# Talking-heads attention with an expert layer: stores of converted weights three slots later, two maxima taken a step later

## The chip, the cores and the metric

The kernel runs on one core of a Trainium2 chip. A core has five engines that run their own instruction queues in order: TensorE (PE, matmuls; PEld its weight loads), VectorE (DVE), ScalarE (ACT), GpSimd (POOL) and SyncE (SP). SP computes nothing here: it issues nearly all DMAs, one after the other, and where one of them has to wait for its data or for room, everything behind it in SP's queue waits too. The metric is the device time of one execution in microseconds (us).

## The reference

Inputs are q, k, v of shape (4 batches, 12 heads, 448 rows, 64), two 12 x 12 matrices that mix heads, and the two weights of the second layer, which arrive as 64-bit floats.

```python
scores = scale * np.matmul(q, k.transpose(0, 1, 3, 2))
scores = np.einsum('bhij,hg->bgij', scores, w_pre)     # mix the heads
scores = scores - np.max(scores, axis=-1, keepdims=True)
attn = np.exp(scores)
attn = attn / (np.sum(attn, axis=-1, keepdims=True) + 1e-09)
attn = np.einsum('bhij,hg->bgij', attn, w_post)        # and again
x = np.matmul(attn, v)                                 # -> (1792, 768)
h = x @ w_in                                           # 768 x 2048
g = np.where(h >= 1, h, np.where(h <= -1, 0.0, (h + 1) ** 2 / 4))
out = g @ w_out                                        # 2048 x 768
```

## The kernel before

**Three stages.** First attention (to about 495 us), then the product with `w_in` and the gate g (to 710.6), then the product with `w_out`. The instructions are issued in an order that the program writes out by hand (`tc.manual_schedule()`): each engine runs its instructions in the order in which the Python code emits them, and a framework adds the waits for data and for free buffers.

**Attention.** A batch's 448 rows are cut into row tiles of 120, 120, 120 and 88 rows. `scores` (L157) multiplies q by k for all heads, ScalarE and VectorE copy the result to `ssb` (L162, L166), and a DMA regroups it (`load_s`, L181, SBUF to SBUF) into blocks of 10 rows x 12 heads, so that mixing heads becomes one 120 x 120 matmul (`pre`, L200 and L202). Every second block is split into a high and a low part by VectorE first (`split`, L189). Then come the row maximum (VectorE, L205), the exponential (ScalarE, L211), the norm (L217, L218 on VectorE, L222 on POOL), the second mixing (`post`, L232, evicted by ScalarE at L234) and the product with v (`pv`, L249). The loop at the end of the attention stage goes over 48 groups, three to a row tile, mostly of four blocks. In each iteration n it emits, in this order: the score loads of group n+1; `pre`, maxima, exponentials and norm of group n; a burst of conversion slots; `post` of group n-1; a row tile's transposes, `pv` and `scores`; loads of k, q and v for later; a second burst of conversion slots. Twelve groups make a batch: v of the next batch is loaded during some of them, k during others.

**The conversion of the weights** runs in these bursts, in groups 2 to 42. The weights are cut into 64 chunks of 128 x 384. For each, `load` (L327) brings the 64-bit floats (384 KB) into `wraw`, of which there are three buffers. Five steps make 32-bit floats in a tile `wt`: step 0 and step 1 on ScalarE (L288 into `wt`, L294 into `wk`), step 2 and 3 on VectorE (L297, L303), step 4 on POOL, an add (L307). `store` (L334) writes the 192 KB back to HBM. A slot is one entry of a list of closures; chunk n begins in slot 3n, and the table `lags` says how many slots later each step comes:

```python
lags = ((store, 8), (4, 6), (2, 4), (3, 4), (1, 3), (0, 2), (load, 0))
```

So the add of chunk n is emitted in slot 3n+6 and its store in 3n+8. Within a slot the order is that of the table. All DMAs named so far are SP's.

**The second stage** is 56 steps j = 7q + k: eight groups q of seven products k = 0 to 6, the first four groups with 512 columns, the others with 384. A step is 18 matmuls (`product`, L509) into one of the accumulators in PSUM named X, Y and Z. Per step the loop emits: the matmuls; `split_w(j + 2)`, which splits the weights of two steps later into a high part (ScalarE, L399) and a low one (VectorE, L402); a gate, in four of the seven steps; sums of weights and x (L435, L464), splits of x (L456, L457); and at the end `evict_f(j)`, which takes the accumulator to SBUF: a copy on ScalarE for k = 0, 2, 3 (L562), an add on VectorE for k = 1, 4, 5 (L564). The matmuls of step k = 6 add to the accumulator that was evicted at k = 4, and therefore wait for that add.

**The gate** g is computed as max(h, f(h)). With `act=True` (k = 3 and k = 4, from the second group on) ScalarE does three operations into a temporary (L536, L543, L544), two temporaries taking turns, and VectorE takes the maximum (L547). VectorE's queue holds the maximum right there, ahead of the sums, splits and evictions of the same step.

Of the kernel before, what the change touches and what calls it, by code (L numbers as in the profile page):

```python
# [9 lines left out]
F32 = mybir.dt.float32  # L10
F32R = mybir.dt.float32r
I32 = mybir.dt.int32
# [3 lines left out]
ALU = mybir.AluOpType  # L16
# [6 lines left out]
def tile_talking_heads_moe(  # L23
# [11 lines left out]
    nc = tc.nc  # L35
# [13 lines left out]
    CW = 384  # L49
# [25 lines left out]
    for b in range(B):  # L75
        for i0 in range(0, S, QT):
            n = min(QT, S - i0)
# [194 lines left out]
    def convert(st, p):  # L272

        def halves():  # L280
            w = st["raw"].bitcast(I32).rearrange("p (n t) -> p n t", t=2)
            return w[:, :, 0], w[:, :, 1]

        def scaled():
            lo, hi = halves()
            if "t" not in st:
                st["t"] = p.tile([128, CW], I32, tag="wt", name="wt", bufs=3)
            nc.scalar.activation(out=st["t"].bitcast(F32), in_=hi.bitcast(F32), func=AF.Copy,  # L288
                                 scale=2.0 ** -111)

        def lowest():
            lo, hi = halves()
            st["k"] = p.tile([128, CW], I32, tag="wk", name="wk", bufs=2)
            nc.scalar.activation(out=st["k"], in_=lo.bitcast(U32), func=AF.Copy, scale=2.0 ** -29)  # L294

        def shifted():
            nc.vector.tensor_single_scalar(out=st["t"], in_=st["t"], scalar=3,  # L297
                                           op=ALU.logical_shift_left)

        def sign():  # L300
            lo, hi = halves()
            t = st["t"]
            nc.vector.scalar_tensor_tensor(out=t, in0=hi, scalar=-0x80000000, in1=t,  # L303
                                           op0=ALU.bitwise_and, op1=ALU.bitwise_or)

        def add():
            nc.gpsimd.tensor_tensor(out=st["t"], in0=st["t"], in1=st.pop("k"), op=ALU.add)  # L307

        return [scaled, lowest, shifted, sign, add]

    def conv_units():
        chunks = []
        for f in range(NF):
            for c in range(2):
                chunks.append((w_in[c * CW:(c + 1) * CW, f * 128:(f + 1) * 128]
                               .rearrange("(k p) f -> p k f", p=128), wsd[f, c]))
            for c in range(2):
                chunks.append((w_out[f * 128:(f + 1) * 128, c * CW:(c + 1) * CW],
                               wod[f, :, c * CW:(c + 1) * CW]))
        st = {}  # L320
        us = []

        def load(n):
            raw = qp.tile([128, CW], I64, tag="wraw", name="wraw", bufs=3)
            src = chunks[n][0]
            dst = raw if len(src.shape) == 2 else raw.rearrange("p (k f) -> p k f", f=128)
            nc.sync.dma_start(out=dst, in_=src)  # L327
            st[n] = {"raw": raw}
            st[n]["steps"] = convert(st[n], qp)

        def store(n):
            dst = chunks[n][1]
            src = st.pop(n)["t"].bitcast(F32)
            nc.sync.dma_start(out=dst, in_=src)  # L334


        lags = ((store, 8), (4, 6), (2, 4), (3, 4), (1, 3), (0, 2), (load, 0))
        for slot in range(3 * len(chunks) + 8):
            def unit(slot=slot):
                for f, lag in lags:  # L340
                    n, rest = divmod(slot - lag, 3)
                    if rest == 0 and 0 <= n < len(chunks):
                        if callable(f):
                            f(n)
                        else:
                            st[n]["steps"][f]()
            us.append(unit)
        return us


    NA = 1024
    NH = (512, 384)
# [6 lines left out]
    raw = {}  # L359
    wts = {}  # L360
    xraw = {}
    xop = {}
    gq = {}
    named = {}
    area = {"gg": 16544, "xd": 82080, "xc": 122848, "xa": 147424}

    def view(p, off, *dims, dt=F32):
        n = 1
        for d in dims:
            n *= d  # L370
        named[p] = named.get(p, -1) + 1
        x = nc.alloc_sbuf_tensor_at(f"{p}_{named[p]}", [128, n], dt, offset=area[p] + off).ap()
        if len(dims) == 2:
            x = x.rearrange("p (a b) -> p a b", b=dims[1])
        return x
# [5 lines left out]
    GHOME = (("xd", 18432), ("xa", 36864), ("xc", 12288), ("xa", 0))  # L381
    SLOT = tuple(("xa", 36864 + 2048 * i) for i in range(7))
    RING = tuple(("xa", 36864 + 1536 * i) for i in range(9)) + tuple(("xd", 24576 + 1536 * i) for i in range(3))
    SUM = ("xd", 29504)
    TEMP = (("xd", 32576), ("xd", 36672))
# [21 lines left out]
    def split_to(t, o=None):  # L407
        return split_hi(t, o)()
# [18 lines left out]
    def split_w(j):  # L427
        if j < NJ:
            wts[j] = split_to(raw[KIND[j % 7], j // 7] if j < NJA else raw.pop(j))

    def sum_w(o, x, y, op, q):
        if o == "S1":
            raw[o, q] = view(*SUM, 2, CW)
        x, y, o = (raw[n, q] for n in (x, y, o))
        nc.vector.tensor_tensor(out=o, in0=x, in1=y, op=op)  # L435

# [6 lines left out]
        return xd[:, 3 * i + r, t0:t0 + NH[ph]]  # L443

    def load_x(name, r, spot, ph):
        xraw[name, r] = view(*spot, NH[ph])
        nc.sync.dma_start(out=xraw[name, r], in_=x_src(name, r, ph))

    def load_xa(name, r, slot):
# [2 lines left out]
    def split_x(x, r, k, ph):  # L452
        p, off = HOMES[ph][k]
        n = NH[ph]
        hi, lo = xop[ph, k, r] = [view(p, off + 8 * n * r + 4 * n * i, n, dt=F32R) for i in range(2)]
        nc.scalar.activation(out=hi, in_=x, func=AF.Copy)  # L456
        nc.vector.tensor_tensor(out=lo, in0=x, in1=hi.bitcast(F32), op=ALU.subtract)  # L457

# [30 lines left out]
    piece = {}  # L489

    def load_xb(p):
        if p < 21:
            k, r = divmod(p, 3)
            piece[p] = view(*RING[p % 12], NH[1])
            nc.sync.dma_start(out=piece[p], in_=x_src(XK[k], r, 1) if k in (0, 1, 5) else xtd[XK[k], r])

    def split_xb(k):
# [28 lines left out]
        return gq[ph, q % NQ].rearrange("p (n i) t -> p n i t", i=2)[:, :, i, h * NH[ph]:(h + 1) * NH[ph]]  # L526

    ngate = [0]

    def gate(src, dst, act):  # L530
        a = dst
        if src is dst:
            n = src.shape[2]
            a = view(*TEMP[ngate[0] % 2], 2, n)
            ngate[0] += 1
        first = nc.scalar.activation(out=a, in_=src, func=AF.Relu, scale=-0.5 if act else 0.5, bias=c05)  # L536
        if ngate[0] == 1:
            for x in kept:
                tc.add_manual_dep(first.ins, x.ins.name,
                                  mybir.DependencyInfo(mybir.DependencyClass.Sync, mybir.DependencyReason.ANTI),  # L540
                                  reason="the last rows of x leave this place")
        if act:
            nc.scalar.activation(out=a, in_=a, func=AF.Relu, scale=-1.0, bias=c1)  # L543
            nc.scalar.activation(out=a, in_=a, func=AF.Square)  # L544
        else:
            nc.vector.scalar_tensor_tensor(out=a, in0=a, scalar=1.0, in1=a, op0=ALU.min, op1=ALU.mult)
        nc.vector.tensor_tensor(out=dst, in0=src, in1=a, op=ALU.max)  # L547

    def gate_slot(q, i, h, act=False):
        d = slot(q, i, h)  # L550
# [22 lines left out]
    tset = {}  # L573
# [20 lines left out]

    def room(tag, m=2):
        i = used[tag] = used.get(tag, -1) + 1
        return view(*ROOM[tag][i % len(ROOM[tag])], m, CW)

    def load_t(i):
        k, z = divmod(i, 4)  # L600
# [8 lines left out]
    def split_t(i):  # L609
        if i >= NTS:  # L610
            return
        t = traw.pop(i)
        if isinstance(t, list):
            nc.vector.tensor_tensor(out=t[0], in0=t[0], in1=t[1], op=ALU.subtract)
            t = t[0]
        tset[i] = split_to(t, None if i % 4 else [view("xc", 3072 * n, 2, CW, dt=F32R) for n in range(2)])

    job = {}

# [23 lines left out]
    def prep_s(j):  # L643
        k, hf, u = items[j]
        src = blk(PROD[k][1], hf, u)
        n = UNITS[u][1]
        hi, lo = (view("xa", 12288 + 8192 * (j % 3) + 4096 * i, 4, 256, dt=F32R)[:, :, :n] for i in range(2))
        nc.scalar.activation(out=hi, in_=src, func=AF.Copy)  # L648
        nc.vector.tensor_tensor(out=lo, in0=src, in1=hi.bitcast(F32), op=ALU.subtract)
        sset[j] = (hi, lo)  # L650
# [60 lines left out]
    with tc.manual_schedule():  # L711
# [46 lines left out]
        for m in groups[0]:  # L758
# [7 lines left out]
            out=wpre.rearrange("p (i g) -> p i g", g=H),  # L766
# [137 lines left out]
                                                      reuse_waits="tile"))  # L904

        for z in range(NQ):
            gq[0, z] = view("gg", 16384 * z, 4, NA)
            gq[1, z] = view(*GHOME[z], 4, 2 * NH[1])
        XAT = {23: 0, 24: 1, 25: 2, 26: 3, 27: 4, 29: 5, 30: 6}
        for j in range(NJ):  # L910
            q, k = divmod(j, 7)
            ph = j // NJA
            end = q == NQ - 1
            if j:
                step(j)
                split_w(j + 2)
            else:
                evict_f(0)
            if k == 0 and q:
# [134 lines left out]
```

## Time and profile before

| | |
|---|---|
| median of 3 runs | 914.97 us (912.14 to 915.5) |
| profiled execution, its own time | 919.67 us |
| its span | 917.8 us |
| busy share of the span | PE 96%, PEld 84%, DVE 74%, ACT 62%, POOL 20% |
| TensorE's granted clock, mean | 0.993 |
| moved by DMA | 162.30 MB, mean 177 GB/s |
| stretches | attention to about 495 us; second stage to 710.6; last product to 917.8 |

Busy times come from a hardware profile of one execution. The ends of matmuls are modelled, so a busy PE need not be at its peak. Where a row gives a wait, "A <- B" reads: A waited, and B's end released it. A wait for several things is put down to the one that came last.

### The profile page before, as it was taken

Reading aid. Unit: us, or ns where it says so; the run is one execution under the profiler, and the core shown is the slowest. Engines: PE = TensorE matmul, PEld = TensorE weight load, DVE = VectorE, ACT = ScalarE, POOL = GpSimd, SP = SyncE. Lnnn points to the kernel's source line nnn. Section 1 sums busy time; section 2 is a strip of 40 time slices with the busy share of each in tenths; the row PEclk is TensorE's granted clock in tenths of the full one; section 3 lists DMA queues with packets and bytes.
Section 4 is the critical chain, followed back from the end, with each engine's and each line's share of the span. In section 5 each row is a group of like instructions: output and inputs, shape, how many; then the busy total and the mean of one; then the engine's idle time right before and its main releaser. Section 6 shows DMA issues by size and latency. Waiting matters only on the chain.

```text
span 917.8 us, 17492 instructions
## 1 busy us (share of the span) xinstructions
PE 877.5 (96%) x6410; PEld 766.4 (84%) x6410; DVE 681.2 (74%) x1121; ACT 565.7 (62%) x1157; POOL 180.3 (20%) x253
## 2 busy tenths in 40 slices
PE   8999999899998999999999999989999999999998
PEld 7787787678776778777888778779998999999998
DVE  4878778688686787758759878877666987868753
ACT  4787677667776767766675566577667444433431
POOL 0334334443443334344321000000000000000000
PEclk9999999999999999999999999999999999999999
DMA  7858677786778796676375744563443545123341
GB/s 169 232 176 239 190 237 238 203 238 202 217 227 224 223 241 194 201 233 197 129 242 140 258 164 146 199 201 117 121 121 100 190 148 174 55 66 109 116 138 60
DMA packets 155832, 162.30 MB, mean 177 GB/s; under 512 B 64100, under 2 KB 149476, under 8 KB 155748
## 3 DMA queue, kind: packets, MB, share of 16 engines
q1 hardware_dynamic: 152964, 160.51, 57.5%
q10 hardware_dynamic: 2784, 0.69, 0.4%
q8 instruction: 51, 0.84, 0.4%
q14 instruction: 33, 0.27, 0.1%
HBM read 88.81 MB, written 33.82 MB: 134 GB/s over the span
## 4 chain that ended last, share of the span: by engine, by line
PE 59%; DMA 14%; ACT 11%; DVE 10%; SPq 3%; issue 3%; POOL 0%; DVEq 0%; ACTq 0%
PE ps_f L665 22%; PE ps_f L509 12%; PE ps_a L232 8%; PE ps_x L249 5%; DMA wraw<-in_moe_w_in_dram 5%; PE ps_l L202 4%; PE ps_s L157 4%; DMA s<-ssb 4%; DMA wraw<-in_moe_w_out_dram 3%; ACT e L211 3%; PE ps_l L200 2%; SPq L181 2%; DMA wi<-wsd 2%; ACT wt L288 1%; DVE wt L303 1%
## 5 line engine op out<-in xcount | busy, mean ns | idle before, releaser
L222 POOL TENSOR_SCALAR wr<-wpost,rs 120x120 f32<-120x120 f32 x180 | 115.1, 655 | 288.9 <-DVE rs L218 211.4
L232 PEld LDWEIGHTS ps_a<-wr,e 120*112 120x112 f32 x1440 | 155.4, 177 | 15.2 <-issue 13.0
L232 PE MATMUL ps_a<-wr,e 120*112 120x120 f32 (+1 forms) x1440 | 158.3, 266 | 6.4 <-ACT e L211 6.1
L665 PE MATMUL ps_f<-wh,xa 128*128 128x384 f32 x588 | 157.2, 334 | 0.0
L211 ACT ACTIVATE e<-ps_l,nm 120x448 f32<-120x448 f32 x180 | 112.5, 631 | 46.2 <-DVE nm L205 45.7
L202 PE MATMUL ps_l<-s,wpre 120*120 120x448 f32 x196 | 97.2, 580 | 13.7 <-DMA s<-ssb 11.8
L665 PEld LDWEIGHTS ps_f<-wh,xa 128*128 128x128 f32 x588 | 106.8, 188 | 0.0
L205 DVE TENSOR_REDUCE nm<-ps_l 120x1 f32<-120x448 f32 x180 | 100.9, 616 | 5.7 <-PE ps_l L202 5.3
L399 ACT ACTIVATE wh<-wi 128x768 fp32r<-128x768 f32 x71 | 59.5, 841 | 65.4 <-PE ps_f L509 23.5
L665 PE MATMUL ps_f<-wl,xa 128*128 128x384 f32 x294 | 98.2, 334 | 0.0
L234 ACT ACTIVATE aT<-ps_a 112x480 f32<-112x480 f32 x180 | 94.2, 588 | 3.3 <-PE ps_a L232 3.1
L509 PE MATMUL ps_f<-xa,wh 128*128 128x384 f32 (+1 forms) x336 | 93.2, 358 | 0.0
L402 DVE SCALAR_TENSOR_TENSOR wl<-wi,wh 128x768 fp32r<-128x768 f32 x71 | 67.7, 954 | 28.5 <-ACT wh L399 28.5
L249 PE MATMUL ps_x<-aT,v 112*64 112x120 f32 (+1 forms) x1536 | 83.5, 262 | 2.0 <-ACT aT L234 1.9
L189 DVE CAST sh<-s 120x448 fp32r<-120x448 f32 (+1 forms) x82 | 31.4, 383 | 67.8 <-DMA s<-ssb 67.7
L249 PEld LDWEIGHTS ps_x<-aT,v 112*64 112x64 f32 x1536 | 73.8, 137 | 8.2 <-ACT aT L234 3.0
L288 ACT ACTIVATE wt<-wraw 128x384 f32<-128x384 f32 x64 | 35.8, 560 | 56.2 <-DMA wraw<-in_moe_w_in_dram 29.9
L307 POOL TENSOR_TENSOR wt<-wt,wk 128x384 int32<-128x384 int32 x64 | 65.2, 1027 | 16.2 <-ACT wk L294 6.9
L509 PEld LDWEIGHTS ps_f<-xa,wh 128*128 128x128 f32 x336 | 61.7, 188 | 5.7
L648 ACT ACTIVATE xa<-gg 128x1024 fp32r<-128x1024 f32 x28 | 29.7, 1060 | 58.5 <-PE ps_f L665 58.3
L166 DVE COPY ssb<-ps_s 120x448 f32<-120x448 f32 (+1 forms) x96 | 56.6, 617 | 7.2 <-PE ps_s L157 7.0
L509 PE MATMUL ps_f<-xa,wl 128*128 128x384 f32 (+1 forms) x168 | 60.6, 361 | 1.1 <-ACT xa L562 1.0
(151 smaller groups left out, 1660.3 us busy)
## 6 DMA issues: line engine op xcount, KB each, us to landing
s<-ssb SPq DMA_DIRECT2D x172, 210.0 KB
wraw<-in_moe_w_in_dram SPq DMA_DIRECT2D x32, 384.0 KB
wraw<-in_moe_w_out_dram SPq DMA_DIRECT2D x32, 384.0 KB
wi<-wod SPq DMA_DIRECT2D x29, 384.0 KB
wi<-wsd SPq DMA_DIRECT2D x28, 384.0 KB
wsd<-wt SPq DMA_DIRECT2D x32, 192.0 KB
wod<-wt SPq DMA_DIRECT2D x32, 192.0 KB
wi<-wss SPq DMA_DIRECT2D x16, 384.0 KB
```

What stands on the lines that cost most here:

```text
L202: nc.tensor.matmul(out=lps[m], lhsT=wpre[:k], rhs=x[:k], start=True, stop=True)
L205: nc.vector.tensor_reduce(out=nm, in_=lps[m], axis=AX.X, op=ALU.max, negate=True)
L211: nc.scalar.activation(out=e, in_=ps, func=AF.Exp, bias=nm, accum_out=sm[:, j:j + 1])
L222: nc.gpsimd.tensor_scalar_mul(out=w[:, :, :ni], in0=wpost[:, :, :ni], scalar1=rs[:, j:j + 1])
L232: nc.tensor.matmul(out=ps[:, r, :ni * H], lhsT=e[:, r * KP:(r + 1) * KP], rhs=w[:, :, :ni], start=True, stop=True)
L234: nc.scalar.activation(out=aT[t][:, :, :, c:c + ni], in_=ps[:, :, :ni * H].rearrange("q r (h i) -> q r h i", h=H), func=AF.Copy)
L249: nc.tensor.matmul(out=ps[s * D:(s + 1) * D, m, :n], lhsT=vt[b, g][:, 2 * m + s, r * D:(r + 1) * D], rhs=a[:, r, 4 * g + 2 * m + s, :n], s ...
L307: nc.gpsimd.tensor_tensor(out=st["t"], in0=st["t"], in1=st.pop("k"), op=ALU.add)
L399: nc.scalar.activation(out=hi, in_=t, func=AF.Copy, scale=2.0 ** -8)
L402: nc.vector.scalar_tensor_tensor(out=lo, in0=t, scalar=2.0 ** -8, in1=hi.bitcast(F32), op0=ALU.mult, op1=ALU.subtract)
L509: nc.tensor.matmul(out=o, lhsT=u[:, c, k], rhs=x, start=first and r == 0 and m == 0, stop=r == 2 and m == 2, skip_group_check=True)
L665: nc.tensor.matmul(out=o, lhsT=x[:, f, c], rhs=y[:, f % 2, :], start=first and f == 0 and m == 0, stop=hf == 1 and f == 3 and m == 2, skip ...
```

## The change

The store of a chunk moves from 8 to 11 slots after the chunk's load, the list of slots gets three more entries, and `wt` gets a fourth buffer. In the second stage, a gate with `act=True` no longer issues its maximum: it puts it on a list, and the list is worked off in the next step, right behind `split_w`. Gates with `act=False` keep theirs in place. The rest of the diff gives the views of SBUF names of their own, at the same addresses.

```diff
-                st["t"] = p.tile([128, CW], I32, tag="wt", name="wt", bufs=3)
+                st["t"] = p.tile([128, CW], I32, tag="wt", name="wt", bufs=4)
...
-        lags = ((store, 8), (4, 6), (2, 4), (3, 4), (1, 3), (0, 2), (load, 0))
-        for slot in range(3 * len(chunks) + 8):
+        lags = ((store, 11), (4, 6), (2, 4), (3, 4), (1, 3), (0, 2), (load, 0))
+        for slot in range(3 * len(chunks) + 11):
...
-    def view(p, off, *dims, dt=F32):
+    def view(name, p, off, *dims, dt=F32):
...
-        named[p] = named.get(p, -1) + 1
-        x = nc.alloc_sbuf_tensor_at(f"{p}_{named[p]}", [128, n], dt, offset=area[p] + off).ap()
+        named[name] = named.get(name, -1) + 1
+        x = nc.alloc_sbuf_tensor_at(f"{name}_p{named[name]}", [128, n], dt, offset=area[p] + off).ap()
...
+    maxima = deque()
...
             nc.scalar.activation(out=a, in_=a, func=AF.Square)
+            maxima.append((dst, src, a))
         else:
             nc.vector.scalar_tensor_tensor(out=a, in0=a, scalar=1.0, in1=a, op0=ALU.min, op1=ALU.mult)
-        nc.vector.tensor_tensor(out=dst, in0=src, in1=a, op=ALU.max)
+            nc.vector.tensor_tensor(out=dst, in0=src, in1=a, op=ALU.max)
+
+    def take_maxima():
+        while maxima:
+            d, x, a = maxima.popleft()
+            nc.vector.tensor_tensor(out=d, in0=x, in1=a, op=ALU.max)
...
                 step(j)
                 split_w(j + 2)
+                take_maxima()
```

## Rows read from the trace of the kernel before

**Rows 1.** The page, busy us, share of the span, instructions of each engine.
```profile
PE 877.5 (96%) x6410; PEld 766.4 (84%) x6410; DVE 681.2 (74%) x1121; ACT 565.7 (62%) x1157; POOL 180.3 (20%) x253
```

**Rows 2.** Stretches: length, busy time of each engine, granted clock, DMA share, GB/s.
```profile
70.28:104.90 34.62, 31.60 (x291) 26.07 (x289) 27.28 (x58) 22.99 (x58) 13.64 (x19) 1.00 0.76 213
...
320.00:340.00 20.00, 18.55 (x172) 14.92 (x171) 17.28 (x38) 12.31 (x30) 8.06 (x11) 1.00 0.94 243
372.23:436.15 63.92, 58.19 (x523) 46.92 (x521) 46.38 (x101) 44.11 (x114) 26.16 (x35) 0.97 0.66 205
495.00:710.60 215.60, 203.90 (x1014) 179.97 (x1010) 161.15 (x188) 137.39 (x199) 0.00 (x0) 0.99 0.51 161
610.60:616.00 5.40, 5.40 (x18) 4.28 (x17) 4.86 (x9) 0.69 (x3) 0.00 (x0) 0.68 0.41 116
710.60:917.80 207.20, 203.84 (x1176) 203.51 (x1175) 152.31 (x160) 79.79 (x94) 0.00 (x0) 1.00 0.36 118
```

**Rows 3.** The chain that ended last, in order of time: start, us, what.
```profile
11.88 1.72 PE ps_k L123 x16
...
420.12 3.28 PE ps_a L232 x32
...
423.63 1.79 PE ps_x L249 x32
...
442.42 1.79 PE ps_x L249 x32
```

**Rows 4.** SP's own waits in 40:445, 372.23:436.15, 313.24:346.89: us, times, longest.
```profile
SPq L334 <- POOL wt L307: 114.9, 33, 10.0
...
SPq L334 <- POOL wt L307: 25.6, 6, 6.0
...
SPq L334 <- POOL wt L307: 1.9, 2, 1.6
```

**Rows 5.** The engines' waits from 40 to 445 us: total, times, longest.
```profile
DVE sh L189 <- DMA s<-ssb: 67.7, 36, 5.5
...
ACT wt L288 <- DMA wraw<-in_moe_w_in_dram: 29.9, 16, 4.4
...
ACT wt L288 <- DMA wraw<-in_moe_w_out_dram: 24.6, 13, 6.3
```

**Rows 6.** Timeline, all engines, 156 to 171 us: start, us, instruction, idle before it.
```profile
156.03 0.33 SPq L116 DMA_DIRECT2D v<-in_v_dram  x1
...
159.98 2.32 POOL L307 TENSOR_TENSOR wt<-wt,wk 128x384 int32<-128x384 int32 x2
...
161.36 0.33 SPq L334 DMA_DIRECT2D wod<-wt  x1
...
166.51 0.39 DVE L189 CAST sh<-s 120x448 fp32r<-120x448 f32 x1 [3.92 <-DMA s<-ssb]
...
170.09 1.35 PE L202 MATMUL ps_l<-s,wpre 120*120 120x448 f32 x2 [2.36 <-DMA s<-ssb]
```

**Rows 7.** Line L547: what its engine waited for before it, us, times.
```profile
  ACT xd L544: 26.6, 13
```

**Rows 8.** Line L564: its widest form (ns), and TensorE's wait for it (us, times).
```profile
L564 DVE TENSOR_TENSOR gg<-ps_f,gg x12: 1216/1218/1219, 504.3 to 612.0; 128x1024 f32<-128x1024 f32 x12
...
  PE ps_f L509: 9.8, 7
```

**Rows 9.** Timeline, all engines, 540 to 549 us.
```profile
541.87 0.96 DVE L402 SCALAR_TENSOR_TENSOR wl<-wi,wh 128x768 fp32r<-128x768 f32 x1
...
545.18 1.23 DVE L547 TENSOR_TENSOR gg<-gg,xd 128x1024 f32<-128x1024 f32 x1 [2.35 <-ACT xd L544]
...
548.07 0.50 PE L509 MATMUL ps_f<-xd,wl 128*128 128x512 f32 x1 [1.17 <-DVE gg L564]
```

**Rows 10.** Timeline, all engines, 602 to 611 us.
```profile
605.89 1.33 ACT L456 ACTIVATE xa<-xa 128x384 fp32r<-128x384 f32 x3
...
609.84 0.50 PE L509 MATMUL ps_f<-xd,wl 128*128 128x512 f32 x1 [2.92 <-DVE gg L564]
```

More of the change, by code (lines that the diff above doesn't have):

```diff
@@ L432, in sum_w @@
         if o == "S1":
-            raw[o, q] = view(*SUM, 2, CW)
+            raw[o, q] = view("s1", *SUM, 2, CW)
         x, y, o = (raw[n, q] for n in (x, y, o))
@@ L445, in load_x @@
     def load_x(name, r, spot, ph):
-        xraw[name, r] = view(*spot, NH[ph])
+        xraw[name, r] = view("xr", *spot, NH[ph])
         nc.sync.dma_start(out=xraw[name, r], in_=x_src(name, r, ph))
@@ L454, in split_x @@
         n = NH[ph]
-        hi, lo = xop[ph, k, r] = [view(p, off + 8 * n * r + 4 * n * i, n, dt=F32R) for i in range(2)]
+        hi, lo = xop[ph, k, r] = [view(f"{'ab'[ph]}{k}{'hl'[i]}", p, off + 8 * n * r + 4 * n * i, n, dt=F32R)
+                                     for i in range(2)]
         nc.scalar.activation(out=hi, in_=x, func=AF.Copy)
@@ L493, in load_xb @@
             k, r = divmod(p, 3)
-            piece[p] = view(*RING[p % 12], NH[1])
+            piece[p] = view("xr", *RING[p % 12], NH[1])
             nc.sync.dma_start(out=piece[p], in_=x_src(XK[k], r, 1) if k in (0, 1, 5) else xtd[XK[k], r])
@@ L533, in gate @@
             n = src.shape[2]
-            a = view(*TEMP[ngate[0] % 2], 2, n)
+            a = view("ga", *TEMP[ngate[0] % 2], 2, n)
             ngate[0] += 1
@@ L596, in room @@
         i = used[tag] = used.get(tag, -1) + 1
-        return view(*ROOM[tag][i % len(ROOM[tag])], m, CW)
+        return view(tag, *ROOM[tag][i % len(ROOM[tag])], m, CW)
     def load_t(i):
@@ L615, in split_t @@
             t = t[0]
-        tset[i] = split_to(t, None if i % 4 else [view("xc", 3072 * n, 2, CW, dt=F32R) for n in range(2)])
+        tset[i] = split_to(t, None if i % 4 else [view("w" + "hl"[n], "xc", 3072 * n, 2, CW, dt=F32R)
+                                                   for n in range(2)])
     job = {}
@@ L646, in prep_s @@
         n = UNITS[u][1]
-        hi, lo = (view("xa", 12288 + 8192 * (j % 3) + 4096 * i, 4, 256, dt=F32R)[:, :, :n] for i in range(2))
+        hi, lo = (view("sg" + "hl"[i], "xa", 12288 + 8192 * (j % 3) + 4096 * i, 4, 256, dt=F32R)[:, :, :n]
+                  for i in range(2))
         nc.scalar.activation(out=hi, in_=src, func=AF.Copy)
@@ L906, in tile_talking_heads_moe @@
         for z in range(NQ):
-            gq[0, z] = view("gg", 16384 * z, 4, NA)
-            gq[1, z] = view(*GHOME[z], 4, 2 * NH[1])
+            gq[0, z] = view("gq", "gg", 16384 * z, 4, NA)
+            gq[1, z] = view("gq", *GHOME[z], 4, 2 * NH[1])
         XAT = {23: 0, 24: 1, 25: 2, 26: 3, 27: 4, 29: 5, 30: 6}
```

## The prediction

> **What bounds the kernel now.** I read the busy shares first: TensorE is busy for 96% of the span, VectorE for 74% [rows 1]. An engine that is busy for 96% leaves 40 us, so whatever this change wins, it wins from stretches in which TensorE waits or runs slowly. The view by stretches places them. The closing product from 710.6 us on loses 3.4 us of 207.2 and none of it is touched. The second stage (the products of the first layer, 495.0 to 710.6) loses 11.7 us of 215.6. The rest lies in the attention stage, in which the weights are converted [rows 2].
>
> For the attention stage I need the pace of a group of four blocks that waits for nothing. The chain of waits gives it: the value product starts at 423.63 and, two groups later, at 442.42, so 9.40 us a group over two groups, with conversion still running [rows 3]. Three stretches of six groups each fall into the time in which v is reloaded; in the first group of each only three blocks are multiplied by the second mixing matrix (8 of 32 matmuls fewer, a quarter of 3.28 us [rows 3]). Undisturbed, such a stretch is 6 x 9.40 - 0.82 = 55.6 us. They took 61.5, 62.6 and 63.9 (the last of the three is in [rows 2]), so 21.2 us are lost in them. Three stretches of three groups reload k and add 24 transposes (16 take 1.72 us [rows 3]): 28.2 + 2.6 = 30.8 us undisturbed, against 34.6, 32.9 and 33.7 (the first is in [rows 2]): 8.8 us lost. The two groups before the first k stretch lose about 1 us, by the same pace.
>
> Why are they late? The waits of SP's own queue name one line: the store of a converted chunk (L334) waited for POOL's add (L307) for 114.9 us, 33 times [rows 4]. Of these 21.8, 14.1 and 25.6 fall in the three v stretches, 61.5 us, and only 1.8, 0.8 and 1.9 in the three k stretches, 4.5 us; the last of either kind stands in [rows 4]. The waits of the engines show what stood behind it: VectorE's split waited 67.7 us for score loads, ScalarE's first conversion step 54.5 us for weight loads [rows 5]. One episode shows the mechanism whole [rows 6]: SP has issued at 156.03 and then stands at the store until POOL's second add ends near 161.3; the store goes at 161.36, and only then a weight load and four score loads. VectorE waits 3.92 us for the first of these at 166.51, and TensorE, after 2.36 us idle, begins the group at 170.09. The waits feed themselves: a weight load that comes late holds ScalarE, then POOL's add, then the next store.
>
> In the second stage VectorE's maximum (L547) waited 13 times, 26.6 us, for ScalarE's square [rows 7], and TensorE waited 9.8 us in 7 places for the eviction L564 that stands behind it [rows 8]. The timeline around 545 us shows the order: the maximum waits 2.35 us, starts at 545.18 and ends at 546.41; a subtraction follows, then L564 of 1.22 us, and TensorE restarts at 548.07 after 1.17 us idle [rows 9]. By these times the subtraction takes 0.4 us.
>
> **The change, part by part.**
>
> Stores three slots later. There are 64 chunks of three slots. The add of chunk n is in slot 3n+6, its store was in 3n+8 and is now in 3n+11. A group takes 200/41 = 4.88 slots (203/41 = 4.95 after), in two bursts. Two slots often fall in the same burst as the add, five never do: the store now stands about a group (9.4 us) behind its add, and the longest of the waits was 10.0 us [rows 4]. So I put the 114.9 us of SP's wait at nearly nothing. On SP the store keeps its place, in slots of residue 2, ahead of the weight load of residue 0; it is a store of a chunk that is one older. No DMA is added, none changes its size. The fourth buffer keeps ScalarE's distance: the tile that step 0 of chunk n+4 overwrites in slot 3n+14 was stored in 3n+11, three slots before, as with three buffers and lag 8. Three more slots in the loop add no work, only 1.5% more of it to a group.
>
> What is that worth? Less than the wait, since most of it (114.9 - 61.5 - 4.5 = 48.9 us) lies in groups that lose next to nothing. In the v stretches the ends are 0 (what is late next is as late) and 21.2 us. I take 0.6 of it, 12.7 us: two of three groups have scores that were written long before, and their loads can go up to a group earlier; every third group is the first of its row tile, its loads must wait for VectorE's last copy of the scores (L166) in the iteration just before, and v itself waits for the value product of its own iteration. In the k stretches SP waits 4.5 us in all, so at most that goes; the transfers are the limit there (DMA share 0.76 in the first, 0.94 at 320 to 340 us [rows 2]). I take half, 2.2 us. With 0.6 us before them the attention stage gives 15.5 us; the ends are 0 and 31 us.
>
> Maxima at the head of the next step. 14 maxima move (two in each of seven groups of steps). Each still costs what it did, 1.23 us at 1024 columns [rows 9], and none is removed: what goes is VectorE's wait. Before, the maximum of step 4 stood ahead of step 4's eviction. After, this eviction stands behind step 3's maximum, whose input is then ready, and step 4's maximum goes behind the next weight split, which waits for ScalarE's hi part, which in ScalarE's order is behind the same square. So the maximum never waits, and the split is no later than before. Worked at 541: split done at 542.8, maximum to 544.0, subtraction to 544.4, eviction to 545.6; TensorE was out of work at 548.07 - 1.17 = 546.9 [rows 9], so the slack is 1.3 us. For six of the seven places I take the whole idle time, 9.8 - 2.9 = 6.9 us. The seventh, at 609.84, differs: splits of x (L457) stand between, and their hi parts come from ScalarE behind the gate too, from 605.89 to 607.22 [rows 10]. VectorE's last split then ends half a us later, near 607.7, where now L564 starts at 609.84 - 1.22 = 608.6: 0.9 us gained of the 2.9, because the wait moves to L457. TensorE's granted clock was 0.68 from 610.6 to 616.0, just after this idle time: most of that stretch at 1.2 instead of 2.4 GHz [rows 2], which cost 5.4 x 0.32 = 1.7 us. Two us of idleness stay, so whether the clock falls is open; I count half, 0.9 us. Sum 8.7 us; the ends are 0 and 11.5 (9.8 + 1.7). A loss has no mechanism here: the moved instruction needs nothing that comes later than what stood ahead of it.
>
> The renaming of the views moves no address and I cost it at nothing.
>
> Sum: 15.5 + 8.7 = 24.2 us. The profiled execution took 919.67 us with a span of 917.8, so 1.9 us lie around it; less 24.2 is 895.5. The median of the runs is 914.97, 4.7 below the profiled one, and the same gain gives 890.8. I say 890.
>
> **The rivals.** (1) The transfers are the limit, and SP gives up one wait for another. For it: share 0.94 at 243 GB/s from 320 to 340, so full engines would carry about 259 GB/s; and v cannot be issued before the value product ends. Against: the share was 0.66 in the last of the v stretches, where most is lost [rows 2]. Then the attention stage gives 0 to 4 us: 904. In the page "DMA: Bandwidth & Descriptors" (Specifications) the Trainium skill gives about 358 GB/s of HBM bandwidth to a core; by that page alone this rival could not occur, and rival 4 with its 872 us would take its chance. The trace does not agree: the row with the share of 0.94 stands for 259 here.
>
> (2) The maxima bring nothing, because VectorE waits for the hi part (L399) where it waited for the square. For it: the split is behind ScalarE too. Against: the 1.3 us of slack above. Only the attention gain stays: 899.
>
> (3) Slower. SP, now free, issues a weight load of 384 KB ahead of the score loads of the first group of a row tile, which VectorE needs at once; at 243 GB/s [rows 2] it holds them for 1.6 us. Before, the late store kept it back. Over 14 tiles that is 22 us, with no other gain in this stage and 8.7 in the next: 928. It decides if the wait of VectorE's split for score loads grows from 67.7 us to more than 76 (the gain of the second part). Against: the order in SP's queue is unchanged, and a load that is issued early has mostly landed by then.
>
> (4) Everything goes: 31 us and 11.5 us: 872. For it: no share of a whole stretch in [rows 2] is above 0.76. Against: the first group of each tile.
>
> **How the numbers follow.** Forecast 0.66, by itself 880 to 899; rival 1 0.16; rival 2 0.08; rival 3 0.05; rival 4 0.05. I can tell a difference of 0.5%, 4.6 us, from none: below 910.4 is faster. Forecast, rivals 2 and 4 and nearly all of rival 1 are faster; its tail, with a small gain in the second stage too, is the same. That gives faster 0.90, same 0.05, slower 0.05. The range 878 to 906 leaves out rivals 3 and 4 and the tails.
>
> **What would show it.** Right: L334's wait for L307 falls from 114.9 us to under 15; the v stretches shrink from about 62.7 us to about 58.5 each, the k stretches by under 1 us each; ScalarE's wait for weight loads falls below 25 us; L547 waits for nothing; TensorE waits for L564 only near 608 us; the second stage is 206 to 208 us long. Wrong: v stretches of the same length with SP waiting elsewhere (rival 1), L564 still waited for, behind L402 (rival 2), longer waits of L189 for scores (rival 3).

## The result, and the profile after

The changed kernel takes 888.18 us (median of 6 runs, 885.92 to 896.4) against 914.84 of the kernel before on the same chip: a ratio of 0.9727, 95% interval 0.9688 to 0.9766. (The ratios here stand as they are on record with their intervals; they differ a little from the quotients of the medians, which give 0.971 here.) The forecast was 890, faster. Its profiled execution took 888.03 us, its span is 886.3.

The page of the changed kernel, busy us, share of the span, instructions ([rows 1] before):

```profile
PE 867.8 (98%) x6410; PEld 763.0 (86%) x6410; DVE 680.0 (77%) x1121; ACT 566.8 (64%) x1157; POOL 178.2 (20%) x253
```

All engines do the same work in a shorter span; TensorE is busy 98% of it instead of 96%. The stretches that answer to [rows 2], the changed kernel (length, busy time of PE, PEld, DVE, ACT, POOL, granted clock, DMA share, GB/s): the first with k, the second and the third with v, the place just behind the gate of the fourth group of steps, the second stage.

```profile
70.08:102.83 32.75, 31.58 (x290) 26.08 (x288) 27.18 (x58) 23.02 (x58) 12.58 (x18) 1.00 0.88 248
242.93:299.37 56.44, 55.59 (x522) 45.85 (x521) 46.33 (x100) 43.88 (x114) 24.36 (x33) 1.00 0.84 250
356.88:413.65 56.77, 55.59 (x522) 45.85 (x521) 46.20 (x100) 43.98 (x112) 25.08 (x34) 1.00 0.75 236
584.00:590.00 6.00, 5.77 (x18) 4.60 (x19) 6.00 (x10) 2.29 (x5) 0.00 (x0) 0.72 0.38 122
472.50:678.90 206.40, 202.07 (x1013) 180.10 (x1008) 160.00 (x188) 137.15 (x199) 0.00 (x0) 0.99 0.53 168
```

A v stretch needs 56.4 to 56.8 us where it took 61.5 to 63.9, and 55.6 was worked out as undisturbed. The same transfers go in less time, at 250 GB/s and a share of 0.84 in the second of these stretches. The second stage has shrunk from 215.6 to 206.4 us.

SP's own waits from 40 to 425 us, changed kernel (against [rows 4]): total us, times, longest.

```profile
SPq L181 <- DVE ssb L166: 50.8, 14, 10.5
SPq L116 <- PE ps_x L249: 30.9, 9, 6.4
SPq L334 <- POOL wt L307: 19.9, 13, 3.8
```

The store's wait for the add fell from 114.9 to 19.9 us (another 3.9 us at the store are put down to POOL's norm, L222). SP is not idle less because of that: it now runs ahead and waits for what really is not there yet, the last copies of the scores (L166, 5.9 us before, over 40 to 445) and the value product that frees v's tile (L249, 7.0 before). Those waits cost little: the v stretches come within about 1 us of undisturbed with them. The engines' waits over the same stretch (against [rows 5]):

```profile
DVE sh L189 <- DMA s<-ssb: 18.1, 18, 1.7
...
ACT wt L288 <- DMA wraw<-in_moe_w_out_dram: 14.5, 6, 3.4
ACT wt L288 <- DMA wraw<-in_moe_w_in_dram: 11.1, 7, 3.1
```

In the second stage the maxima now have the line L555, the eviction L572. No idle time stands before L555. TensorE waits for L572 once instead of 7 times (us, times; against [rows 8]), and the timeline shows where (against [rows 10]): the last row is TensorE's restart.

```profile
  PE ps_f L510: 2.2, 1
```

```profile
581.00 1.33 ACT L457 ACTIVATE b2h_p<-xr_p 128x384 fp32r<-128x384 f32 x3
...
581.54 1.49 DVE L458 TENSOR_TENSOR b2l_p<-xr_p,b2h_p 128x384 fp32r<-128x384 f32 x3 [1.64 <-ACT b2h_p L457]
...
582.96 1.22 DVE L572 TENSOR_TENSOR gq_p<-ps_f,gq_p 128x1024 f32<-128x1024 f32 x1
...
584.23 0.50 PE L510 MATMUL ps_f<-a6h_p,wl 128*128 128x512 f32 x1 [2.20 <-DVE gq_p L572]
```

Now VectorE waits 1.64 us for the splits of x there, where it waited for the square in the kernel before:

```profile
606.02 1.23 DVE L547 TENSOR_TENSOR gg<-gg,xd 128x1024 f32<-128x1024 f32 x1 [2.36 <-ACT xd L544]
```

### The profile page after: what moved, and what is told of

Same layout as the page of the kernel before. It is cut to its first block, busy times and chain, and to the rows that moved or that the text cites. A ratio compares the mean times of both kernels' runs of the same rounds, so it can differ in the third digit from the quotient of the medians.

```text
span 886.3 us, 17512 instructions
## 1 busy us (share of the span) xinstructions
PE 867.8 (98%) x6410; PEld 763.0 (86%) x6410; DVE 680.0 (77%) x1121; ACT 566.8 (64%) x1157; POOL 178.2 (20%) x253
## 2 busy tenths in 40 slices
DMA packets 155832, 162.30 MB, mean 183 GB/s; under 512 B 64100, under 2 KB 149476, under 8 KB 155748
## 4 chain that ended last, share of the span: by engine, by line
PE 82%; DMA 9%; ACT 4%; DVE 2%; SPq 2%; issue 1%; POOL 0%; ACTq 0%; DVEq 0%
PE ps_f L675 23%; PE ps_f L510 22%; PE ps_a L232 12%; PE ps_x L249 7%; PE ps_l L202 6%; PE ps_s L157 6%; PE ps_l L200 4%; DMA wraw<-in_moe_w_in_dram 3%; DMA s<-ssb 3%; DMA wraw<-in_moe_w_out_dram 2%; ACT e L211 1%; SPq L181 1%; PE ps_t L140 1%; ACT wt L288 1%; DMA qraw<-in_q_dram 1%
## 5 line engine op out<-in xcount | busy, mean ns | idle before, releaser
L222 POOL TENSOR_SCALAR wr<-wpost,rs 120x120 f32<-120x120 f32 x180 | 114.0, 649 | 264.1 <-DVE rs L218 212.7
L232 PEld LDWEIGHTS ps_a<-wr,e 120*112 120x112 f32 x1440 | 155.0, 177 | 12.8 <-issue 10.7
L658 ACT ACTIVATE sgh_p<-gq_p 128x1024 fp32r<-128x1024 f32 (+1 forms) x56 | 53.3, 953 | 90.8 <-PE ps_f L675 90.6
L675 PE MATMUL ps_f<-wh,sgl_p 128*128 128x384 f32 x294 | 98.2, 334 | 0.0
L675 PE MATMUL ps_f<-wh,sgh_p 128*128 128x384 f32 x294 | 98.2, 334 | 0.0
L675 PE MATMUL ps_f<-wl,sgh_p 128*128 128x384 f32 x294 | 98.2, 334 | 0.0
L202 PE MATMUL ps_l<-s,wpre 120*120 120x448 f32 x196 | 94.1, 563 | 0.2 <-DMA s<-ssb 0.2
L659 DVE TENSOR_TENSOR sgl_p<-gq_p,sgh_p 128x1024 fp32r<-128x1024 f32 (+1 forms) x56 | 60.9, 1088 | 35.8 <-ACT sgh_p L658 35.8
L249 PE MATMUL ps_x<-aT,v 112*64 112x120 f32 (+1 forms) x1536 | 83.5, 262 | 1.5 <-ACT aT L234 1.4
L249 PEld LDWEIGHTS ps_x<-aT,v 112*64 112x64 f32 x1536 | 73.8, 137 | 7.6 <-ACT aT L234 2.7
L166 DVE COPY ssb<-ps_s 120x448 f32<-120x448 f32 (+1 forms) x96 | 57.3, 619 | 17.2 <-PE ps_s L157 17.1
L162 ACT ACTIVATE ssb<-ps_s 120x448 f32<-120x448 f32 (+1 forms) x96 | 51.9, 548 | 17.3 <-PE ps_s L157 14.3
L200 PE MATMUL ps_l<-sh,wpre_h 120*120 120x448 f32 (+1 forms) x82 | 58.6, 715 | 0.0
L190 DVE TENSOR_TENSOR sl<-s,sh 120x448 fp32r<-120x448 f32 (+1 forms) x82 | 54.2, 662 | 2.8
L675 PEld LDWEIGHTS ps_f<-wh,sgh_p 128*128 128x128 f32 x294 | 55.2, 188 | 0.0
```

The lines of the kernel that those rows point to most:

```text
L200: nc.tensor.matmul(out=lps[m], lhsT=w[:k], rhs=y[:k], start=(j == 0), stop=(j == 2))
L202: nc.tensor.matmul(out=lps[m], lhsT=wpre[:k], rhs=x[:k], start=True, stop=True)
L222: nc.gpsimd.tensor_scalar_mul(out=w[:, :, :ni], in0=wpost[:, :, :ni], scalar1=rs[:, j:j + 1])
L232: nc.tensor.matmul(out=ps[:, r, :ni * H], lhsT=e[:, r * KP:(r + 1) * KP], rhs=w[:, :, :ni], start=True, stop=True)
L249: nc.tensor.matmul(out=ps[s * D:(s + 1) * D, m, :n], lhsT=vt[b, g][:, 2 * m + s, r * D:(r + 1) * D], rhs=a[:, r, 4 * g + 2 * m + s, :n], s ...
L675: nc.tensor.matmul(out=o, lhsT=x[:, f, c], rhs=y[:, f % 2, :], start=first and f == 0 and m == 0, stop=hf == 1 and f == 3 and m == 2, skip ...
```

## The experiments

For every kernel I read two lengths: the time at which TensorE begins the last group of attention (its first mixing matmul, L202), and the time from there to the first matmul of the last product (the "tail" below). The last product took 204.0 to 204.1 us in all of them. Theory H: SP's queue stood at the store, and loads that others needed came late behind it; and VectorE stood at the maximum, and the eviction that TensorE needed came late behind it. Both are the same thing, a queue worked off in order with a waiting instruction ahead of work that is wanted sooner.

**The kernel before, once more.**

> The kernel before, profiled once more. Its profiled execution was 4.7 us above its median, and the two profiles differ by 31.6 us where the medians differ by 26.7. If the attention stage varies from run to run, this profile shows v stretches that add up to something other than 188.0 us, and the second stage the same to 0.5 us; if the profiled execution is slow as such, all stretches are as before.

It took 914.58 us, span 912.6. The stretches from the start of the last attention group to the last product, first the kernel before, then this run:

```profile
470.28:710.42 240.14, 228.32 (x1288) 201.23 (x1287) 181.35 (x222) 155.72 (x239) 4.40 (x6) 0.99 0.50 158
```

```profile
464.95:705.26 240.31, 228.48 (x1289) 201.41 (x1288) 181.32 (x222) 155.82 (x239) 4.39 (x6) 0.99 0.50 157
```

The tail is the same to 0.2 us, the attention stage 5.3 us shorter; its v stretches took 61.8, 60.2 and 61.4 us, together 183.4 instead of 188.0. So the attention stage varies from one execution to the next, and of the two profiles the prediction read the longer. Against this second one, the changed kernel is 26.3 us shorter in span (912.6 - 886.3), which is what the medians say (26.7).

**One part at a time.**

```diff
 e1_stores_only
-            maxima.append((dst, src, a))
+            nc.vector.tensor_tensor(out=dst, in0=src, in1=a, op=ALU.max)
 e2_maxima_only
-                st["t"] = p.tile([128, CW], I32, tag="wt", name="wt", bufs=4)
+                st["t"] = p.tile([128, CW], I32, tag="wt", name="wt", bufs=3)
...
-        lags = ((store, 11), (4, 6), (2, 4), (3, 4), (1, 3), (0, 2), (load, 0))
-        for slot in range(3 * len(chunks) + 11):
+        lags = ((store, 8), (4, 6), (2, 4), (3, 4), (1, 3), (0, 2), (load, 0))
+        for slot in range(3 * len(chunks) + 8):
```

> The stores' part alone: lag 11 and four buffers, the maxima where they were. Theory H (SP stood at the store, and everything behind it in SP's queue came late): the attention stage is as short as in the changed kernel, the second stage as long as before (about 9 us longer), so 888.2 + 9.2 = about 897. Its rival D (the gain is in the second stage, and the attention stage differs from run to run): about 905 or more. If the two parts need each other, it is outside 894 to 901.

> The maxima alone: lag 8 and three buffers. If the second stage's gain of 9.2 us stands by itself: 914.8 - 9.2 = about 905.6, TensorE waits for the eviction L572 once (near the splits of x) instead of 7 times, and SP's wait at the store stays at about 115 us. If VectorE only waits elsewhere (for the hi part of the weights): no change, 914.

Stores alone: 901.49 us, ratio 0.9885 (0.9816 to 0.9955). Maxima alone: 900.52 us, ratio 0.9872 (0.9790 to 0.9953). Their tails:

```profile
451.26:691.43 240.17, 228.14 (x1288) 201.80 (x1287) 181.10 (x222) 155.71 (x239) 4.40 (x6) 0.99 0.50 157
```

```profile
464.51:694.09 229.58, 225.37 (x1288) 200.34 (x1287) 179.98 (x222) 155.66 (x239) 4.40 (x6) 1.00 0.52 165
```

The parts are separate: with the stores alone the tail is as before, and TensorE waited for L572 7 times, 9.8 us, as before; with the maxima alone the attention stage ends as late as in the second profile of before (464.5 against 465.0), and SP's wait at the store is still there (40 to 430 us; 108.6 in the kernel before over that stretch):

```profile
SPq L334 <- POOL wt L307: 102.7, 31, 10.0
```

Of the two times the first is half a us outside what I expected, the second 5 us below it, with the kernel before between 905.5 and 917.7 beside them: the times alone carry the two parts to a few us, the traces better. The two ratios multiply to 0.976, where the whole change gave 0.973 and, on this chip, 0.975 (below). Both kernels have the renamed views, and in each the untouched stage is as long as before, so the renaming cost nothing that shows.

**Lag and buffer apart.**

```diff
 e3_three_buffers
-                st["t"] = p.tile([128, CW], I32, tag="wt", name="wt", bufs=4)
+                st["t"] = p.tile([128, CW], I32, tag="wt", name="wt", bufs=3)
 e10_buffer_only: the lag back to 8 as in e2_maxima_only, bufs=4 stays
 e7_lag14
-                st["t"] = p.tile([128, CW], I32, tag="wt", name="wt", bufs=4)
+                st["t"] = p.tile([128, CW], I32, tag="wt", name="wt", bufs=5)
...
-        lags = ((store, 11), (4, 6), (2, 4), (3, 4), (1, 3), (0, 2), (load, 0))
-        for slot in range(3 * len(chunks) + 11):
+        lags = ((store, 14), (4, 6), (2, 4), (3, 4), (1, 3), (0, 2), (load, 0))
+        for slot in range(3 * len(chunks) + 14):
```

> The changed kernel with three buffers for the converted tile instead of four. Step 0 of a chunk then overwrites a tile whose store is issued in the same slot, just ahead of it, so ScalarE must wait for that store to land, some us each time, with the exponentials behind it. If the fourth buffer is needed: 893 to 910 and ScalarE's wait at L288 for the store shows in the waits (over 40 us). If the buffer is only a reserve: 888.

> The fourth buffer alone, with lag 8, and the maxima as in the changed kernel. Theory H: SP stands at the store as before (about 105 us), so the time is that of the maxima alone, 900 to 906. Rival (the buffer alone frees ScalarE): 888 to 895.

> The changed kernel with lag 14 and five buffers: three more slots between add and store. SP's remaining wait at the store, 19.9 us, should go to zero. If some of the attention stage's remaining loss (about 3 us in the stretches with v, 5 in those with k) hangs on it: 1 to 4 us faster, 884 to 887. If it is covered: 888 and no difference.

Three buffers with the late store: 910.04 us, ratio 0.9962 (0.9925 to 0.9999). Its profile is the shortest of its ten runs, 904.58 us. Even there, while the tail is 229.55, so that the gain of the maxima is there, the attention stage ends at 465.84: nothing is left of the stores' gain, and by the median even some of the maxima's is gone. ScalarE's waits in this kernel, 40 to 430 us:

```profile
ACT wt L288 <- DMA wod<-wt: 34.2, 18, 3.2
...
ACT wt L288 <- DMA wsd<-wt: 24.4, 17, 3.5
```

SP waits only 21.5 us at the store, as in the changed kernel, but ScalarE waits 58.6 us for stores to land, with the exponentials behind it. The head of the queue has moved from SP to ScalarE. The buffer alone does it neither: 897.55 us, ratio 0.9835 (0.9797 to 0.9874), SP waits 105.4 us at the store, attention ends at 462.6 in a profile of 901.36 us, the longest of its four runs. The median lies 2.5 us under my lower bound, which came from the maxima alone, and as far above the rival's range. It is 3 us under the median of the maxima alone, and the two intervals overlap; that the buffer by itself gives about so much is not excluded.

Lag 14 with five buffers: 888.71 us, ratio 0.9739 (0.9689 to 0.9789). SP's waits at the store, 40 to 430 us:

```profile
SPq L334 <- POOL wr L222: 9.7, 15, 2.8
SPq L334 <- POOL wt L307: 4.9, 8, 1.5
```

The wait for the add falls from 19.9 to 4.9 us, part of it now put down to the norm, together from 23.8 to 14.6. The ratio is that of the changed kernel within the intervals, and attention ends at 450.8, no earlier than in the changed kernel (447.8 and 447.3 in its two profiles). So this rest was covered.

**The store on another queue.**

```diff
 both kernels; e4_store_on_pool has lag 8 and three buffers as in e2_maxima_only
-            nc.sync.dma_start(out=dst, in_=src)
+            nc.gpsimd.dma_start(out=dst, in_=src)
 e9_pool_behind_add, with four buffers
-        lags = ((store, 11), (4, 6), (2, 4), (3, 4), (1, 3), (0, 2), (load, 0))
-        for slot in range(3 * len(chunks) + 11):
+        lags = ((4, 6), (store, 6), (2, 4), (3, 4), (1, 3), (0, 2), (load, 0))
+        for slot in range(3 * len(chunks) + 8):
```

> Lag 8 and three buffers, but the store is issued from POOL's queue, right behind the add it waits for; the maxima as in the changed kernel. Theory H: nothing stands in SP's queue any more, although the store leaves as early as before, so about 888 (884 to 892). Rival B (the fourth buffer or the later store is what helps, by giving ScalarE's first step more distance or by spreading the transfers): it stays with the maxima alone, about 905. Rival P (a DMA issued by POOL delays POOL's norm and add): over 895, with a longer wait of TensorE for the second mixing.

The first form was slower than the kernel before: 922.26 us, ratio 1.0113 (1.0041 to 1.0184), with the tail of the changed kernel (231.1) and attention ending at 482.2. Theory H as it stood missed it, and so did rival B. Rival P had the side right (over 895), so the question is whether issuing from POOL costs by itself. POOL's timeline and ScalarE's waits show another reason:

```profile
159.12 2.41 POOL L222 TENSOR_SCALAR wr<-wpost,rs 120x120 f32<-120x120 f32 x4 [3.06 <-DVE rs L218]
161.48 0.60 POOL L334 DMA_DIRECT2D wsd<-wt  x1
162.11 1.02 POOL L307 TENSOR_TENSOR wt<-wt,wk 128x384 int32<-128x384 int32 x1
```

```profile
ACT wt L288 <- DMA wod<-wt: 28.8, 11, 5.1
ACT wt L288 <- DMA wsd<-wt: 28.2, 12, 4.9
```

The store's data had been ready since an add of the burst before (155.05 to 156.06), but in POOL's queue it stands behind the next norm (L222), which waits for the sums of the exponentials. It goes at 161.48, and ScalarE, three buffers later, waits 57 us in all for such stores to land. The queue was another one, the place in it no better. So the second form puts the store directly behind the add and keeps the fourth buffer.

> The store once more on POOL's queue, now emitted directly behind its add (lag 6), with four buffers, the maxima as in the changed kernel. In the earlier run the store stood a burst behind its add, behind the next norm in POOL's queue, and ScalarE waited 57 us for its landing. Theory H, mended (what costs is a store that stands in a queue ahead of work that others need, be it SP's or POOL's, or whose landing ScalarE needs at once): none of this is left, so as the changed kernel, 885 to 892, with ScalarE's wait for stores under 10 us. Rival P (stores issued by POOL cost by themselves, 64 x 0.6 us in POOL's queue ahead of the norm): over 895.

891.35 us, ratio 0.9756 (0.9721 to 0.9792): theory H as mended. Rival P with its 895 and more is out, with the same number of stores issued by POOL; a cost of a us or two is not excluded (the changed kernel took 890.26 on this chip, below). Attention ends at 451.7, the tail is 229.6, ScalarE waits for no store. SP has no store in its queue and waits, from 40 to 430 us, mostly where it waits in the changed kernel, and longer for VectorE to release a buffer of `wraw` (L303, 6.0 us in the changed kernel):

```profile
SPq L181 <- DVE ssb L166: 58.9, 14, 10.5
SPq L116 <- PE ps_x L249: 37.6, 9, 7.3
SPq L327 <- DVE wt L303: 26.3, 13, 4.2
```

A store that leaves early from a queue where nothing stands ahead of it and one that leaves late from SP come to about the same time. It is the place in the queue that counts, not the hour at which the bytes go. The two forms on POOL differ in the place and in the number of buffers; what the place alone would do with three buffers was not run.

**The eviction.** Here the maxima stay in their gates, where VectorE waits for them, and only the eviction of product 4 goes ahead of the gate and the splits; in the next two, the maxima are as in the changed kernel and the eviction goes ahead of the splits of x, or ahead of gate, sums and splits.

```diff
 e6_evict_before_gate (maxima in place) and e12_evict_first (maxima a step later)
+            if j and k == 4:
+                evict_f(j)
             if k == 0 and q:
                 gate_slot(q - 1, 1, 0)
...
-            if j:
+            if j and k != 4:
                 evict_f(j)
 e5_evict_before_split: the first two lines stand ahead of "if j in XAT:" instead
```

> The maxima stay in their gates and VectorE waits for ScalarE's square as before, but the eviction of product 4 is emitted ahead of the gate and of the splits; stores as in the changed kernel. If what counts is only that nothing that waits stands ahead of this eviction: as fast as the changed kernel with the eviction ahead of the splits, 884 to 889, with about 25 us of VectorE's wait at the maximum still there. If VectorE's idle time itself costs: about 897, as with the stores alone.

> The changed kernel, with the eviction of product 4 (L572) ahead of the splits of x in the same step. It concerns one place, near 584 us, where TensorE was idle for 2.2 us and then ran at a granted clock of 0.72 for 6 us (1.7 us lost). If the splits' wait for ScalarE holds the eviction: the idle time goes and the clock stays at 1.0, 3 to 4 us faster than the changed kernel, about 884.5. If VectorE is late there for another reason: no change.

886.45 us, ratio 0.9708 (0.9649 to 0.9768), with the maxima in place. This is the row that decides, the maximum with the idle time before it (line, engine, operation, count, busy us, mean ns, idle us):

```profile
L547 DVE TENSOR_TENSOR gq_p<-gq_p,ga_p 128x1024 f32<-128x1024 f32 (+1 forms) x14 | 15.3, 1092 | 19.7 <-ACT ga_p L546 19.7
```

```profile
450.45:678.44 227.99, 225.10 (x1288) 200.44 (x1287) 180.65 (x222) 155.62 (x239) 4.39 (x6) 1.00 0.52 166
```

VectorE still waits 19.7 us at the maxima, and the tail is 228.0, the shortest of all. VectorE's idle time cost nothing by itself; the eviction behind it did. With the eviction ahead of the splits: 886.63 us, ratio 0.9715 (0.9673 to 0.9757), tail 228.55. The idle time at 584 us is gone there, but the time is 2 us above the 884.5 that I expected and not distinguishable from the changed kernel.

> The changed kernel itself, beside the other kernels of this chip: 888, 0.9727 of the kernel before.

> The changed kernel with the eviction of product 4 emitted right behind the maxima, ahead of the gate, of the sums and of the splits of x. The one place where TensorE still waits for that eviction (2.2 us and a clock of 0.72 behind it) should be gone: second stage about 228.5 us instead of 231.1 from the last attention group on, and 2 to 4 us faster than the changed kernel on the same chip, near 886.

On one chip the changed kernel took 890.26 us (0.9747, 0.9714 to 0.9780) and the kernel with the eviction first 887.67 (0.9722, 0.9691 to 0.9753). The median gain of 2.6 us lies in the 2 to 4 that I expected, but the intervals overlap, and the tails differ by only 1.05 us (228.53 against the 229.58 of this profile of the changed kernel). The place at 584 us is clean, with the clock at 1.00, but five steps on TensorE waits again, here first with the eviction first, then in the kernel with the maxima in place:

```profile
601.67 0.41 PE L510 MATMUL ps_f<-b4h_p,wl 128*128 128x384 f32 x1 [1.17 <-DVE wl L402]
```

```profile
602.01 0.41 PE L510 MATMUL ps_f<-b4h_p,wl 128*128 128x384 f32 x1 [0.61 <-DVE wl L402]
```

From 583.3 us on VectorE works through this stretch without a pause, splits of x, low parts of weights and the rest. TensorE, no longer held at 584, runs ahead of it and gives part of the gain back: 2.20 - 1.17 = 1.03 us stay with the eviction first and 2.20 - 0.61 = 1.59 with the maxima in place, and by 1.05 and 1.59 us their tails (228.53 and 227.99) are shorter than 229.58.

## Why the prediction was right

- **Head of SP's queue.** Right, and shown from both sides (stores alone; the store behind its add on POOL). The wait at the store was put at nearly nothing, under 15 us; it was 19.9, and lag 14 showed that this rest is covered. ScalarE's wait for weight loads, put below 25 us, was 25.6 (14.5 + 11.1). In the episode at 156 us it was the first of the two adds in the row, not the second, that ended near 161.3 and released the store; the argument is the same with it.
- **v stretches.** The term was 12.7 us. Against the profile that it was worked out from, 18.1 us went (188.0 to 169.9); against the second profile of the kernel before, 13.5 (183.4 to 169.9). The choice of 0.6 rested on the tile's first group and on v keeping their delay. They do (50.8 and 30.9 us of SP's waits), yet the stretches come to within 1.2 us of undisturbed: this delay was cheaper than I took it to be. The 0.6 was a choice, and too low.
- **k stretches.** 2.2 us forecast, with "at most" the 4.5 us of SP's wait: 32.75, 32.73 and 32.18 against 34.62, 32.94 and 33.65, so 3.5 us. Two of the three shrank by more than the 1 us that was to be the most (1.9, 0.2 and 1.5).
- **The fourth buffer** was called the thing that keeps ScalarE's distance. Shown: without it ScalarE waits 58.6 us and the gain in attention is gone.
- **The maxima.** 8.7 us forecast: the tail fell by 9.0 us (240.1 to 231.1) in the first profiles, and by 10.7 (240.3 to 229.6) in the second ones, where the changed kernel had no low clock. Six places clean, the seventh with 2.2 us of idle time, where 2.0 were worked out, and behind the splits of x as forecast. The half of the clock's cost that I counted as gained was a coin's throw: the clock behind that place was 0.72 in one profile of the changed kernel and 1.00 in the other, and the tails are these:

```profile
447.78:678.88 231.10, 226.66 (x1289) 201.53 (x1287) 180.37 (x222) 155.46 (x239) 4.40 (x6) 0.99 0.52 163
447.29:676.87 229.58, 225.09 (x1288) 200.41 (x1287) 179.97 (x222) 155.64 (x239) 4.40 (x6) 1.00 0.52 164
```

- **Conversion to the median.** Sum and medians agree (24.2 against 26.7; the ratio gives 25.0) in part by luck. Profile against profile the gain was 31.5 us (917.8 - 886.3): the profile of the kernel before was long by some 5 us, which made the loss to be won back look larger, and the attention term took too little of it. The two errors cancel.
- **The rivals.** Rival 1 took the row with a share of 0.94 at 243 GB/s for a limit of 259. The v stretches shrank all the same, to 250 GB/s at 0.84, so no such limit held them. What a given share carries differs from stretch to stretch; the rows are the changed kernel inside a v stretch and the kernel before in its second stage. So a share read in one stretch is no limit for another; that the mix of transfers makes the difference is likely, but no run tested it.

```profile
280.00:290.00 10.00, 9.15 (x89) 7.70 (x87) 8.29 (x18) 6.74 (x18) 3.89 (x6) 1.00 1.00 268
...
520.00:530.00 10.00, 10.00 (x45) 8.23 (x44) 9.32 (x11) 5.56 (x7) 0.00 (x0) 1.00 0.97 347
```

- The Trainium skill's figure of about 358 GB/s of HBM bandwidth to a core ("DMA: Bandwidth & Descriptors", Specifications) is nearly met by the last row, with 347 GB/s. The prediction's "the trace does not agree" set one mix of transfers against that figure, and these GB/s count all transfers, those from SBUF to SBUF too (of the 162.30 MB that the kernel before moved, 122.63 MB were read from or written to HBM).
- Rival 2: VectorE's wait for the hi part did grow (31.2 to 45.6 us), but nothing that TensorE needed at once stood behind it. Rival 3: VectorE's wait for scores fell from 67.7 to 18.1 us. Rival 4, in which everything goes: against undisturbed the k stretches still lose 5 us and the v stretches 3.

## What to carry to other kernels

Where an engine or SP works off a queue in order, ask of each waiting instruction not how long it waits but what stands behind it and who wants that first: the 104 to 115 us of SP's wait at the store were worth some 14 to 23 us of the attention stage, depending on the profiles compared, the 19.7 us that VectorE kept waiting in one experiment nothing. The store went later here at no cost because the tile it empties got one more buffer; lag and buffer belong together, and either alone gave little or nothing. Moving the store to another engine's queue helped only at a place in that queue where nothing that waits stood ahead of it.

## What the runs showed of the hardware that was not expected

TensorE's granted clock fell in some executions of a kernel and not in others, at the same place and after the same idle time: 2.20 us idle near 584 us gave 0.72 over the next 6 us in one profile of the changed kernel, and no low clock at all in its second profile (tails 231.1 and 229.6). Eight profiles have this idle time of 2.2 us at this place, those of all kernels whose second stage is that of the changed one. Three show a low clock behind it, with tails of 231.10 to 231.15 us; five show none, with tails of 229.55 to 229.58. So the low clock cost 1.5 us there, where 1.7 were worked out.

In the attention stage, the first profile of the kernel before has three 10 us stretches with a clock of 0.83 (from 170, 280 and 410 us), its second profile one (from 280), the changed kernel none in either. They do not explain the 5.3 us by which the two attention stages of the kernel before differ. The stretch from 170 lies in a v stretch that took 61.5 us with it and 61.8 without; only the one from 410 lies in a v stretch that was longer with it (63.9 against 61.4), and there TensorE also waited:

```profile
170.00:180.00 10.00, 9.16 (x63) 7.21 (x65) 6.94 (x18) 4.22 (x12) 2.27 (x4) 0.83 0.87 251
410.00:420.00 10.00, 7.72 (x56) 5.27 (x56) 6.45 (x16) 4.19 (x12) 3.67 (x5) 0.83 0.70 209
```

What makes the attention stage vary stays open. A single profile was 4.7 us off the median of its kernel here (919.67 against 914.97), so a sum that is worked out from one profile can carry an error of that size.
